# Issuing every engine's instructions in source order in a decode-attention kernel

## The chip, the cores and the metric

The kernel runs on one core of one Trainium2 chip. A core has a matrix engine (TensorE, PE in the profile, with PEld for its weight loads), a vector engine (VectorE, DVE), an activation engine (ScalarE, ACT), GpSimd (POOL) and a sync engine (SyncE, SP) that here issues the loads. Every engine works through one list of its own instructions, and waits at each for the semaphores that the instruction names. The metric is the device time of one execution in microseconds (us); three executions of the kernel before took 269.32 to 269.83 us, with a median of 269.36 us.

## The reference: what is computed

One token of each of two sequences (B = 2, model width D = 448) goes through a layer with two parallel branches, both fed by the normalised input:

```
xn  = layernorm(x)
q   = xn @ wq                                   # 16 query heads of 256
A   = softmax(q . k^T / 16) . v, then @ wo      # last 4096 cached positions, 8 KV heads
h   = xn @ w1 + b1
B   = (h * tanh(softplus(h))) @ w2              # hidden width 1792
out = x + A + B
```

Two query heads share one KV head. K and V are cut to the last 4096 of 32768 positions, which is 4096 x 256 bf16 numbers for each of 8 KV heads, 2 sequences, K and V: 67.1 MB. With the weights 77.67 MB are read. The output is 2 x 448 numbers.

## The kernel before, in words

**Steps.** There are 16 (KV head, sequence) pairs, and each is cut into two halves of 2048 positions: 32 steps. In the source one pass of the loop at L427 does the following for step `s`: it asks for a later K and V (`load_k(s + 3)`, `load_v(s + 1)`), turns the next step's K (`turn(s + 1)`), makes this step's scores (`scores(s)`) and then works on the values of the step before (`values(s - 1)`). At the 4th pass the dense weights are asked for, at the 10th and 12th the dense branch is computed.

**One step's chain of data.** `load_k` (L303) brings 1 MB of K. `turn` (L330) is a DVE transpose of it in 32x32 blocks (`kt<-k`). `scores` (L339) is eight PE matmuls of 128x512 with the spread-out query `qdiag` as weights (`sc<-kt,qdiag`); ACT then takes the exponential and its row sums (L349, `p<-sc`). `values` transposes the probabilities on DVE (L362, `pT<-p`) and multiplies them with V, which serves as weights, in 32 small PE matmuls (L384, `o<-pT,v`). After a pair's second half two matmuls sum the denominators (L371, `den`), DVE takes the reciprocal (L379) and scales the result (L397, `oT`); after both sequences of a KV head four matmuls add it, through `wo`, to the output sum `psA` (L408). The dense branch is L246 to L278, and its second matmul, into the same `psA`, L283.

**Buffers.** K and V have six tiles each, the turned K three, the probabilities, their transposes, the scores and the attention sums two each. A load into a tile waits until its last reader is through: K's last reader is the `turn` on DVE six steps earlier, V's the value matmuls on PE six steps earlier.

**What sets the order.** The program is written with the Tile framework. It notes which instruction reads and writes what; at the end a scheduler takes the instructions out of a heap by priority and decides for each engine in which order they stand, within these dependencies; semaphores are put in after that. So an engine's list needs not follow the source. SP's list before has the same order as the source: K three steps ahead, V one step ahead. Each load also waits for the load eight places before it in the list of loads, so at most eight are under way.

Of the kernel before, what the change touches and what calls it, by code (L numbers as in the profile page):

```python
# [11 lines left out]
BF16 = mybir.dt.bfloat16  # L12
FP32 = mybir.dt.float32
PSUM = bass.MemoryType.PSUM


@with_exitstack
def kernel(
# [49 lines left out]
    small = ctx.enter_context(tc.tile_pool(name="small", bufs=3))  # L68
    ps_sc = ctx.enter_context(tc.tile_pool(name="ps_sc", bufs=2, space=PSUM))
    ps_o = ctx.enter_context(tc.tile_pool(name="ps_o", bufs=2, space=PSUM))  # L70
    ps_den = ctx.enter_context(tc.tile_pool(name="ps_den", bufs=1, space=PSUM))
    ps_a = ctx.enter_context(tc.tile_pool(name="ps_a", bufs=1, space=PSUM))
    ps_m = ctx.enter_context(tc.tile_pool(name="ps_m", bufs=2, space=PSUM))

# [375 lines left out]
    nc.vector.tensor_copy(out=res[:, 0 : D // 2], in_=psA[:, 0 : D // 2])  # L450
    nc.scalar.copy(out=res[:, D // 2 : D], in_=psA[:, D // 2 : D])
    nc.sync.dma_start(out=out.flatten_outer_dims(), in_=res[:])


# [28 lines left out]
```

## Time and profile before

| | before |
|---|---|
| median of 3 runs | 269.36 us (269.32 to 269.83) |
| profiled execution, its own time | 269.08 us |
| span of that execution (first to last instruction) | 267.3 us |
| mean granted TensorE clock | 0.66 |
| PE busy | 167.8 us, 63% of the span |
| DVE busy | 103.8 us, 39% |
| ACT, POOL busy | 25.4 us, 26.8 us |
| read from memory | 77.67 MB, 291 GB/s over the span |

The profiled execution lies 0.28 us under the median, and 1.78 us of its time lie outside the span. Busy time is a sum over stages; how long an engine sat idle, and on whom, is in the views of waits and of groups of instructions. A profile names an instruction by its source line; lines of the changed kernel are 17 higher, since a function of 17 lines stands ahead of them.

### The profile page before, as it was taken

What the parts mean: (1) busy time and instruction counts of PE and PEld (TensorE: products, weight loads), DVE (VectorE), ACT (ScalarE), POOL (GpSimd) and SP (SyncE); (2) the same over time, 40 slices, a digit from 0 to 9 for tenths busy, and PEclk for the clock granted to TensorE, in tenths of its full rate; (3) what the DMA queues carried; (4) which work ended last, traced back from release to release, by engine and by line L of the source; (5) the groups of instructions that cost most, each with busy time, mean ns of one, the idle gap of its engine ahead of it and who ended that gap; (6) DMA issues with size and microseconds to landing.
All of it is one profiled execution on the core that took longest, in us unless ns stands there. A gap on an engine that the chain in (4) does not pass through costs nothing.

```text
span 267.3 us, 3777 instructions
## 1 busy us (share of the span) xinstructions
PE 167.8 (63%) x1577; PEld 80.4 (30%) x1577; DVE 103.8 (39%) x137; ACT 25.4 (10%) x69; POOL 26.8 (10%) x138
## 2 busy tenths in 40 slices
PE   1259557758447895584557865584576955575765
PEld 0233313326213342242123332241232321232323
DVE  5166442241542244634435044634325144444221
ACT  4002111011011011111111101111110011111100
POOL 5043020020020020202020100202020020000000
PEclk9999855557575586579575557568565557559556
DMA  7999999999999999699887966699886914400000
GB/s 278 417 420 418 417 418 427 415 412 421 423 412 422 418 400 343 264 337 362 312 316 265 363 215 223 264 348 350 310 283 237 362 67 157 157 2 0 0 2 0
DMA packets 12554, 77.90 MB, mean 291 GB/s; under 512 B 1269, under 2 KB 3321, under 8 KB 4090
## 3 DMA queue, kind: packets, MB, share of 16 engines
q1 hardware_dynamic: 12532, 77.67, 75.4%
q8 instruction: 12, 0.20, 0.3%
q14 instruction: 4, 0.03, 0.0%
q10 hardware_dynamic: 6, 0.01, 0.0%
HBM read 77.67 MB, written 0.00 MB: 291 GB/s over the span
## 4 chain that ended last, share of the span: by engine, by line
PE 58%; DVE 25%; issue 8%; DMA 4%; ACT 3%; SPq 0%; ACTq 0%; DVEq 0%
PE sc L339 39%; DVE kt L330 20%; PE o L384 10%; DMA wq_sb<-in_A_wq_dram 4%; PE psA L408 4%; DVE pT L362 4%; ACT p L349 3%; PE den L371 1%; PE psA L283 1%; PE hT_ps L246 1%; PE qT_ps L192 1%; PE hT_ps L255 1%; DVE rec L379 0%; DVE qrep L207 0%; SPq L86 0%
## 5 line engine op out<-in xcount | busy, mean ns | idle before, releaser
L339 PE MATMUL sc<-kt,qdiag 128*128 128x512 bf16 x256 | 109.1, 569 | 62.5 <-DVE kt L330 47.3
L330 DVE STREAM_TRANSPOSE kt<-k 128x2048 f32<-128x2048 f32 x32 | 72.3, 2275 | 0.0
L362 DVE STREAM_TRANSPOSE pT<-p 128x512 bf16<-128x512 bf16 x32 | 22.7, 711 | 107.0 <-ACT p L349 104.8
L339 PEld LDWEIGHTS <-qdiag 128*128 128x128 bf16 x256 | 26.2, 122 | 100.2 <-issue 68.2
L221 POOL COPY qdiag<-qrep 32x8 bf16<-32x8 bf16 x128 | 23.0, 185 | 188.3 <-PE sc L339 170.5
L349 ACT ACTIVATE p<-sc 128x512 bf16<-128x512 f32 x32 | 19.1, 597 | 228.0 <-PE sc L339 228.0
L384 PEld LDWEIGHTS <-v 128*128 128x128 bf16 x1024 | 33.6, 104 | 15.0 <-issue 13.2
L384 PE MATMUL o<-pT,v 128*128 128x2 bf16 x1024 | 32.2, 165 | 0.0
L371 PE MATMUL den<-hsel,rs 128*128 128x2 f32 x64 | 15.1, 305 | 22.6 <-ACT p L349 22.6
L371 PEld LDWEIGHTS den<-hsel,rs 128*128 128x128 f32 x64 | 12.5, 242 | 45.8 <-ACT p L349 45.6
L397 DVE TENSOR_TENSOR oT<-o,rec 128x4 bf16<-128x4 f32 x16 | 2.6, 165 | 36.9 <-PE o L384 36.9
L408 PE MATMUL psA<-wo,oT 128*2 128x448 bf16 x32 | 10.8, 478 | 0.3 <-DVE oT L397 0.3
L192 PE MATMUL qT_ps<-xs,wq_sb 128*128 128x4 bf16 x112 | 3.3, 166 | 5.8 <-DMA wq_sb<-in_A_wq_dram 5.8
L349 ACT ACTIVATION_READ_ACCUMULATOR p<-sc 128x1 f32 x32 | 6.2, 194 | 0.0
L192 PEld LDWEIGHTS <-wq_sb 128*128 128x128 bf16 x112 | 3.1, 104 | 6.4 <-DMA wq_sb<-in_A_wq_dram 6.4
L408 PEld LDWEIGHTS <-oT 128*2 128x2 bf16 x32 | 2.4, 94 | 7.9 <-DVE oT L397 5.0
L283 PE MATMUL psA<-w_sb,act_bf 128*2 128x448 bf16 x14 | 3.7, 413 | 0.0
L246 PE MATMUL hT_ps<-xs,w_sb 128*128 128x4 bf16 x49 | 3.7, 195 | 0.0
L146 PE MATMUL xnT_ps<-ident,xn_bf 2*128 2x2 bf16 x7 | 0.5, 166 | 5.0 <-DVE xn_bf L131 5.0
L246 PEld LDWEIGHTS <-w_sb 128*128 128x128 bf16 x49 | 3.2, 151 | 0.1
L201 DVE CAST qT<-qT_ps 128x64 bf16<-128x64 f32 x1 | 0.2, 225 | 7.2 <-PE qT_ps L192 7.2
L110 POOL MEMSET qdiag<- 128x1024 bf16 x3 | 2.7, 951 | 0.0
(40 smaller groups left out, 20.3 us busy)
## 6 DMA issues: line engine op xcount, KB each, us to landing
k<-in_A_k_cache_dram SPq DMA_DIRECT2D x32, 1024.0 KB, 9.8
v<-in_A_v_cache_dram SPq DMA_DIRECT2D x31, 1024.0 KB, 7.4
wo<-in_A_wo_dram SPq DMA_DIRECT2D x8, 448.0 KB, 18.1
w_sb<-in_B_w_dram SPq DMA_DIRECT2D x2, 1568.0 KB, 22.8
wq_sb<-in_A_wq_dram SPq DMA_DIRECT2D x1, 2048.0 KB
wq_sb<-in_A_wq_dram SPq DMA_DIRECT2D x1, 1536.0 KB, 10.9
v<-in_A_v_cache_dram SPq DMA_DIRECT2D x4, 256.0 KB, 3.4
x_bf<-in_A_x_dram ACTq DMA_DIRECT2D x1, 1.8 KB
```

What stands on the lines that cost most here:

```text
L110: nc.gpsimd.memset(t[:], 0.0)
L192: nc.tensor.matmul(qT_ps[:, hh, e, :], lhsT=wq_v[:, s, hh, e, :], rhs=xs[:, s, :, :].rearrange("p x b -> p (x b)"), start=(s == 0), stop=( ...
L221: nc.gpsimd.tensor_copy(out=tv[rows, :, e, j * Q : j * Q + rep], in_=qrep[rows, :, h0 : h0 + rep, e, x, b],)
L246: nc.tensor.matmul(hT_ps[:, c, :, :].rearrange("p x b -> p (x b)"), lhsT=w1_v[:, s, c, :], rhs=xs[:, s, :, :].rearrange("p x b -> p (x b)" ...
L283: nc.tensor.matmul(psA[:, :], lhsT=act_bf[:, c, x, :], rhs=w2_sb[:, x, c, :], start=False, stop=False, skip_group_check=True,)
L330: nc.vector.transpose(out=kt[:].bitcast(FP32), in_=k_t.pop(s)[:].bitcast(FP32))
L339: nc.tensor.matmul(psc[:], lhsT=qdiag[i % NW][:, n * NE + e, :], rhs=ktv[:, n, e, :, :], start=(n == 0 and e == 0), stop=(n == NB - 1 and ...
L349: nc.scalar.activation(out=p_sb[:], in_=psc[:].rearrange("p t c -> p (t c)"), func=ACT.Exp, scale=scale, accum_out=state["rs", i][:, s % N ...
L362: nc.vector.transpose(out=pT[:], in_=p_t.pop(s)[:])
L371: nc.tensor.matmul(den[:], lhsT=rs[:, n : n + 1].to_broadcast([P, P]), rhs=hsel[:], start=(n == 0), stop=(n == NH - 1),)
L384: nc.tensor.matmul(po[:, c, :], lhsT=vv[:, t, c, :], rhs=pTv[:, t, 0:rep], start=(half == 0 and t == 0 and c == 0), stop=(half == NH - 1 a ...
L408: nc.tensor.matmul(psA[:, :], lhsT=oT[:, c, h, :], rhs=w[:, h, c * D : (c + 1) * D], start=False, stop=(kvh == Hkv - 1 and h == rep - 1 an ...
```

## The change

A new function walks over all recorded instructions in the order in which the source made them. To each it adds a dependency on the instruction before it on the same engine, of the kind that needs no semaphore. The scheduler then has no choice left: each engine's list is the source order. The function is called once, as the last statement of the kernel. No instruction is added to the program or taken out of it, no buffer, wait count or size is edited.

```diff
+def issue_in_order(tc):
+
+    last = {}
+    for ins in tc.nc.cur_bb.bb.instructions:
+        before = last.get(ins.engine)
+        if before is not None:
+            tc.add_manual_dep(
+                ins,
+                before.name,
+                mybir.DependencyInfo(
+                    mybir.DependencyClass.NoSync, mybir.DependencyReason.DATA
+                ),
+                reason="issue_in_order",
+            )
+        last[ins.engine] = ins
...
     nc.sync.dma_start(out=out.flatten_outer_dims(), in_=res[:])
+    issue_in_order(tc)
```

**DVE in the loop.** This is DVE's list in the middle of the loop, before. Numbers behind names tell the tiles of different steps apart; `p_1174` are the probabilities of the scores made from `kt_1101`, `p_1234` those from `kt_1163`, `p_1293` those from `kt_1223`.

```order
L330 STREAM_TRANSPOSE kt_1101<-k_954 128x2048
L362 STREAM_TRANSPOSE pT_1176<-p_1112 128x512
L397 TENSOR_TENSOR oT_1019<-o_1040,rec_1120 128x4
L362 STREAM_TRANSPOSE pT_1237<-p_1174 128x512
L330 STREAM_TRANSPOSE kt_1163<-k_1021 128x2048
L379 RECIPROCAL rec_1242<-den_1239 128x2
L362 STREAM_TRANSPOSE pT_1295<-p_1234 128x512
L330 STREAM_TRANSPOSE kt_1223<-k_1087 128x2048
```

And this is the same place in the changed kernel.

```order
L347 STREAM_TRANSPOSE kt_1163<-k_1021 128x2048
L379 STREAM_TRANSPOSE pT_1176<-p_1112 128x512
L347 STREAM_TRANSPOSE kt_1223<-k_1087 128x2048
L379 STREAM_TRANSPOSE pT_1237<-p_1174 128x512
L396 RECIPROCAL rec_1242<-den_1239 128x2
L414 TENSOR_TENSOR oT_1276<-o_1178,rec_1242 128x4
L347 STREAM_TRANSPOSE kt_1282<-k_1159 128x2048
L379 STREAM_TRANSPOSE pT_1295<-p_1234 128x512
```

Before, the K of the next scores (`kt_1163`) is turned behind the transpose of the probabilities of the scores before them (`p_1174`). Now that same K stands two transposes of probabilities earlier, ahead of `pT_1176`, and `oT` follows its reciprocal directly and stands ahead of the next `turn`.

**PE in the loop.** This is PE's list before; of a run of like rows the first or last is shown, and "..." stands for the others. `sc_1225` and `sc_1284` are the scores of two successive steps, and `pT_1237` are the probabilities of the step before `sc_1225`.

```order
L339 MATMUL sc_1225<-kt_1163,qdiag1_131 128x512
L371 MATMUL den_1360<-hsel_124,rs_1235 128x2
L339 MATMUL sc_1284<-kt_1223,qdiag1_131 128x512
...
L384 MATMUL o_1178<-pT_1237,v_1089 128x2
L339 LDWEIGHTS qdiag1_131
L339 MATMUL sc_1284<-kt_1223,qdiag1_131 128x512
```

The changed kernel, one step later in the program:

```order
L356 MATMUL sc_1346<-kt_1282,qdiag2_133 128x512
L388 MATMUL den_1360<-hsel_124,rs_1235 128x2 x2
L401 LDWEIGHTS v_1213
L401 MATMUL o_1297<-pT_1358,v_1213 128x2
...
L425 MATMUL psA_164<-wo_759,oT_1276 2x448
L356 LDWEIGHTS qdiag2_133
L356 MATMUL sc_1408<-kt_1344,qdiag2_133 128x512
```

Before, the values lie in the middle of a later step's eight score matmuls, and a denominator matmul, which needs the row sums of the scores just made, stands between two steps' scores. Now the eight scores stand together, both denominator matmuls follow the scores of the next step, and `psA` follows the values directly.

**DVE at the start.** Before:

```order
L118 BN_STATS stats<-x_bf 2x6
L120 BN_AGGR mv<-stats 2x2
L125 RECIPROCAL rstd<-rstd 2x1
L131 TENSOR_SCALAR xn_bf<-x_bf,mv,rstd 2x4x128
L131 TENSOR_SCALAR xn_bf<-x_bf,mv,rstd 2x3x128
L97 COPY spread<-ident 32x32 x16
```

The changed kernel:

```order
L114 COPY spread<-ident 32x32 x16
L118 CAST hsel<-ident 128x2
L120 TENSOR_TENSOR hsel<-hsel,ident 128x2 x3
L131 MEMSET eps_t 2x1
L135 BN_STATS stats<-x_bf 2x6
L137 BN_AGGR mv<-stats 2x2
```

The constants `spread` and `hsel` now stand ahead of the layer norm. SP's list, and so the order of all loads, is the same in both kernels. On ACT the dense branch's exponential moves from behind the 7th to behind the 10th exponential of scores.

## The prediction

> **What bounds the kernel now.** First the page's slices of the span, for a first picture: who is busy when.
>
> ```profile
> span 267.3 us, 3777 instructions
> PE   1259557758447895584557865584576955575765
> PEclk9999855557575586579575557568565557559556
> DMA  7999999999999999699887966699886914400000
> ```
>
> PE is half busy all along, at a clock that is mostly at half. The DMA engines are full for some 100 us, then not. The loads are thus not what sets the end. The stretches say it in numbers (columns: length, busy time and count of PE, PEld, DVE, ACT, POOL, clock, DMA share, GB/s).
>
> ```profile
> 0.00:7.00 7.00, 0.95 (x8) 0.41 (x8) 3.87 (x25) 2.86 (x3) 3.84 (x10) 1.00 0.77 284
> 7.00:100.00 93.00, 60.54 (x594) 31.12 (x595) 35.01 (x46) 7.10 (x21) 11.18 (x64) 0.69 1.01 417
> 100.00:210.00 110.00, 70.22 (x621) 32.27 (x620) 45.26 (x44) 10.31 (x30) 10.35 (x56) 0.64 0.84 303
> ```
>
> From 7 to 100 us loads run at 417 GB/s; then at 303. The waits of SP's queue (total us, times, longest) say why they fall.
>
> ```profile
> SPq L314 <- PE o L384: 66.2, 22, 9.1
> SPq L303 <- DVE kt L330: 53.4, 11, 5.4
> ```
>
> Loads wait for tiles: V for the value matmuls, K for the turn. Compute is the slow side, and the chain of waits shows how one step goes.
>
> ```profile
> 129.92 0.04 DVE pT L362
> 129.96 0.60 issue
> 130.56 2.28 DVE kt L330
> 132.88 1.89 PE sc L339 x4
> 134.77 0.83 PE o L384 x32
> 135.60 1.57 PE sc L339 x4
> 137.22 0.47 issue
> 137.69 0.20 ACT p L349
> 137.91 0.71 DVE pT L362
> ```
>
> One step takes 137.91 - 129.92 = 7.99 us, and everything in it is in series: transpose of probabilities, turn of the next K, scores, exponential, transpose. The groups (busy, mean ns of one, idle before and its releaser) confirm it.
>
> ```profile
> L339 PE MATMUL sc<-kt,qdiag 128*128 128x512 bf16 x256 | 109.1, 569 | 62.5 <-DVE kt L330 47.3
> L330 DVE STREAM_TRANSPOSE kt<-k 128x2048 f32<-128x2048 f32 x32 | 72.3, 2275 | 0.0
> L362 DVE STREAM_TRANSPOSE pT<-p 128x512 bf16<-128x512 bf16 x32 | 22.7, 711 | 107.0 <-ACT p L349 104.8
> ```
>
> The turn never waits (0.0 idle before it): its K landed long ago, and it starts when the transpose of probabilities ahead of it in DVE's list is done. DVE sits 107.0 us at that transpose, waiting for ACT, with a turn behind it that could run. Then PE waits for the turn. The order of DVE's list, not data, closes the ring.
>
> **The change part by part.**
>
> *The turn moves ahead (DVE), the values behind whole scores (PE).* In the new order the turn for step s+1 stands in front of the transpose for step s-1, and PE does scores(s), then values(s-1). While PE makes scores(s), DVE turns and transposes; nothing of one step's series of 7.99 us remains in series except as fill. What a step costs now is the largest of three rates, per KV head (four steps). For PE I need the durations at both clocks.
>
> ```profile
> 236.27 2.60 PE sc L339 x6
> 240.01 0.89 PE sc L339 x4
> 150.25 1.58 PE psA L408 x4
> 153.58 0.59 PE L371 MATMUL den<-hsel,rs 128*128 128x2 f32 x2 [0.78 <-ACT p L349]
> 242.07 0.46 PEld L408 LDWEIGHTS <-oT 128*2 128x2 bf16 x4 [0.42 <-DVE oT L397]
> ```
>
> At half clock a score matmul is 2.60/6 = 0.433 us, at full clock 0.89/4 = 0.22. PE at half: 32 scores 13.9, four values at 0.83 = 3.3, two pairs of den 1.2, psA 1.58 and the wait for oT in front of it, now uncovered, 0.42: 20.4 us per head. DVE: four turns 9.1, four transposes 2.8, and under 0.7 for rec and oT: 12.6 us. Its new head-of-line wait, oT for the values on PE, holds the next turn back, but that turn is needed only a step later: after oT come 2.28 + 0.71 = 3.0 us to the next values, under 8 x 0.433 = 3.5 us of scores at half clock (at full clock PE would wait about a microsecond; it then has time). Loads: eight of 1.0486 MB and one wo of 0.459 MB, 8.85 MB at 417 GB/s = 21.2 us per head. So the loads become the bound, by 0.8 us over PE at half clock.
>
> The clock: in the chain above PE's longest wait in the step is the turn's, 132.88 - 130.56 = 2.3 us, and in the slices the clock still sits at half for most of the span. I do not count on the full clock. [...]
>
> *What the loads then take.* 284 GB/s x 7 us = 1.99 MB in the first 7 us; the other 75.68 MB at 417 GB/s take 181.5 us: to 188.5 us. A load lands a little after its bytes' turn:
>
> ```profile
> 1.20 10.86 DMA wq_sb<-in_A_wq_dram
> 12.11 3.05 PE qT_ps L192 x108
> 18.57 1.44 PE sc L339 x3
> ```
>
> wq (3.67 MB) had landed at 12.06, when 1.99 + 2.11 = 4.10 MB had moved: 0.43 MB or 1.0 us of lag. The last V lands at T = 189.5 us. Could the loads still be held? K is asked for three steps ahead into six tiles, so load_k(s+3) waits for turn(s-3), and for the load eight places before it, about K(s-1); while the turns follow the landings within two steps, 10.6 us, no load waits for a tile. The dense branch is such a delay:
>
> ```profile
> 63.27 0.49 PE L246 MATMUL hT_ps<-xs,w_sb 128*128 128x4 bf16 x7
> 67.66 0.26 PE L255 MATMUL hT_ps<-ones,b_sb 1*128 1x2 bf16 x2
> L283 PE MATMUL psA<-w_sb,act_bf 128*2 128x448 bf16 x14 | 3.7, 413 | 0.0
> ```
>
> It takes 4.65 us and, at half clock with psA's 1.58/4 a matmul, 14 x 0.395 = 5.5 us, but its weights also gave PE 3.21 MB = 7.7 us in which no K came. It fits.
>
> *The end.* Behind K(31) in the list are three V loads, 3.15 MB = 7.5 us. So K(31) lands at T - 7.5, is turned by T - 5.2, pT(29) ends at T - 4.5, values(29) at T - 3.7, scores(31) at half clock at T - 0.2, exponential (0.7) and pT(31) (0.71) at T + 1.2, values(31) at T + 2.0. From there it is the old end:
>
> ```profile
> 262.69 0.18 DVE oT L397
> 262.91 1.48 PE psA L408 x4
> 265.18 0.33 SPq L452 DMA_DIRECT2D out_dram<-res  x1
> ```
>
> 267.3 - 262.7 = 4.6 us. Span: 189.5 + 2.0 + 4.6 = 196.1 us; with scores at full clock 1.89 instead of 3.46, 194.5.
>
> *The start.* spread and hsel (DVE) move ahead of the layer norm.
>
> ```profile
> 5.09 1.62 DVE L97 COPY spread<-ident 32x32 bf16<-32x32 bf16 x16
> 7.60 0.34 DVE L162 TENSOR_SCALAR xs<-xnT_ps,odd 128x6 bf16<-128x6 bf16 x2
> ```
>
> That is 1.62 + 0.17 + 0.45 = 2.2 us ahead of xs, which is ready at 7.94 and needed, with wq, at 12.06: 4.1 us of cover. Zero. Without cover it would be 2.2 us on PE's start, still under the loads. PE's first scores stay at 18.57. ACT's and POOL's lists have 0.8 and under 1 us per step: zero.
>
> *Sum.* The profiled execution has 269.08 - 267.3 = 1.78 us outside the span: 196.1 + 1.8 = 197.9. The median lay 0.28 above the profiled execution; **I predict 198 us**, 26% less.
>
> **The rivals.**
>
> *PE's ring decides (A).* PE stays at half clock and each hand-over costs more than in my sum. PE's sum without loads: 18.6 + 8 x 20.4 + 4.65 + 5.5 + 4.6 = 197, already level with the loads; 0.1 to 0.3 us per step for hand-overs and 2 to 4 us of DVE standing at the dense branch give 201 to 210 us, say 205 with the outside. For: the chain's "issue" pieces of 0.47 us. Against: where PE had no pause it was granted nearly the full clock (0.91):
>
> ```profile
> 95.00:100.00 5.00, 5.00 (x52) 2.41 (x50) 2.95 (x3) 0.00 (x0) 0.65 (x4) 0.91 0.99 388
> ```
>
> *The loads are slower than 417 (B).* After 100 us the DMA engines were 84% busy for 303 GB/s, 303/0.84 = 361 GB/s of busy time, where the early stretch gives 417/1.01 = 413. If that is the rate of transfers beside dense compute, and not an artefact of few loads under way, then 75.68 MB / 361 = 210 us, T = 217.7, time 226. Against: in the early stretch PE was as busy (60.54 of 93 us against 70.22 of 110) and the rate held. [...]
>
> *Slower than before (C).* DVE's list now has a turn, which needs a K from memory, ahead of the transpose of probabilities that are ready. If K is late, values wait, V tiles stay taken, and SP, stuck at the V load, does not ask for the next K. Such a ring would pay a whole K load per step:
>
> ```profile
> k<-in_A_k_cache_dram SPq DMA_DIRECT2D x32, 1024.0 KB, 9.8
> ```
>
> 18.6 + 32 x 9.8 + 4.6 + 1.8 = 339 us. It beats 269 from (267.3 - 18.6 - 4.6)/32 = 7.6 us per step on, that is, if a K is asked for less than 9.8/7.6 = 1.3 steps before its turn. Against: it is asked for three steps ahead, and six tiles allow it.
>
> *The order was not what held it (D).* 269 us, if the turn needs something that comes late anyway. The 0.0 idle ahead of the turn and the DVE rows speak against it.
>
> **How the numbers follow.** Forecast (loads bound, 195 to 201): 0.70. A (201 to 210): 0.17. B (210 to 230): 0.07. C: 0.03. D: 0.03. The range from 194.5 to 208 takes in the forecast, both clocks, a load rate from 425 to 400 GB/s (-3 to +8 us) and most of A. A measurement of this kernel tells 0.2% from no change. Faster: 0.70 + 0.17 + 0.07 = 0.94; with D split into 0.02 same and a sliver either way, faster 0.95, same 0.02, slower 0.03.
>
> **What would show it.** Right: the DMA slices at 9 up to about 188 us with about 417 GB/s; SP's waits are for other loads, those for PE o and DVE kt nearly gone; turns now sit idle waiting for DMA k; PE's idle time ahead of scores no longer goes to DVE kt behind pT; the last V lands some 6 us before the span's end. A shows as PE near 9 in every slice, SP again waiting for PE o, and a clock at 0.5. B shows as a DMA share of 1.0 at about 360 GB/s. C shows as K loads issued one at a time. I am wrong about the step if PE and DVE still alternate while loads wait.

## The result, and the profile after

The changed kernel takes 199.02 us in the median of four executions (197.60 to 199.63), the kernel before beside it 269.36; the ratio is 0.738 with a 95% interval of 0.733 to 0.743. Medians here and below leave out executions more than 1.5% above the fastest of their kernel, here one of four of the kernel before (273.73 us). The forecast was 198 us. The profiled execution, the fastest of the four, took 197.60 us with a span of 195.8.

First the slices of the page of the changed kernel, and its stretches (columns as in the prediction).

```profile
span 195.8 us, 3758 instructions
PE   0253955699108789999997597489962976597983
PEclk9999999658855756657999969955885698769696
DMA  6999999999999999999999999999999999999950
```

```profile
7.00:100.00 93.00, 67.26 (x733) 38.53 (x734) 47.35 (x60) 10.75 (x29) 11.73 (x73) 0.78 1.01 418
100.00:180.00 80.00, 59.96 (x688) 33.98 (x687) 46.88 (x48) 11.01 (x32) 9.18 (x56) 0.81 1.02 419
180.00:196.00 16.00, 10.90 (x158) 6.76 (x156) 6.58 (x11) 2.40 (x7) 0.00 (x0) 0.79 0.55 221
```

The DMA engines are full to about 188 us, at 418 and 419 GB/s, where they fell to 303 before. SP's waits and the groups show the reversal.

```profile
SPq L320 <- DMA v<-in_A_v_cache_dram: 50.1, 24, 2.2
SPq L331 <- DMA k<-in_A_k_cache_dram: 46.4, 22, 2.3
SPq L331 <- PE o L401: 1.1, 4, 0.3
```

```profile
L347 DVE STREAM_TRANSPOSE kt<-k 128x2048 f32<-128x2048 f32 x32 | 73.7, 2306 | 50.6 <-DMA k<-in_A_k_cache_dram 50.5
L356 PE MATMUL sc<-kt,qdiag 128*128 128x512 bf16 x256 | 83.9, 485 | 2.7 <-DVE kt L347 2.7
L379 DVE STREAM_TRANSPOSE pT<-p 128x512 bf16<-128x512 bf16 x32 | 21.5, 672 | 1.7 <-ACT p L366 1.7
```

Loads now wait for earlier loads; the wait for value matmuls fell from 66.2 to 1.1 us. The turn, which never waited, now waits 50.5 us for K to land. PE's wait for turns fell from 47.3 to 2.7 us, DVE's wait for exponentials from 104.8 to 1.7. The end of the chain of waits:

```profile
164.91 18.67 DMA k<-in_A_k_cache_dram
...
183.61 2.31 DVE kt L347
185.92 0.59 DVE pT L379
...
186.58 0.93 PE o L401 x32
187.50 1.77 PE sc L356 x8
...
189.30 0.70 ACT p L366 x2
...
190.02 0.71 DVE pT L379
...
190.79 0.94 PE o L401 x32
...
191.76 0.18 DVE oT L414
```

The last K lands at 183.6, and from there a chain of single steps leads to the end.

### The profile page after: what moved, and what is told of

The parts are those of the page before. It is cut to its first block, busy times and chain, and to the rows that moved or that the text cites. A ratio compares the mean times of both kernels' runs of the same rounds, so it can differ in the third digit from the quotient of the medians.

```text
span 195.8 us, 3758 instructions
## 1 busy us (share of the span) xinstructions
PE 138.1 (71%) x1577; PEld 79.3 (40%) x1577; DVE 105.9 (54%) x137; ACT 25.4 (13%) x69; POOL 24.7 (13%) x138
## 4 chain that ended last, share of the span: by engine, by line
DMA 89%; DVE 5%; PE 3%; SPq 1%; ACT 1%; issue 0%
DMA k<-in_A_k_cache_dram 40%; DMA v<-in_A_v_cache_dram 30%; DMA wo<-in_A_wo_dram 19%; DVE kt L347 4%; PE o L401 1%; DVE pT L379 1%; PE sc L356 1%; SPq L320 1%; PE psA L425 0%; ACT p L366 0%; SPq L104 0%; SPq L103 0%; DVE res L467 0%; ACT res L468 0%; DVE rec L396 0%
## 5 line engine op out<-in xcount | busy, mean ns | idle before, releaser
L347 DVE STREAM_TRANSPOSE kt<-k 128x2048 f32<-128x2048 f32 x32 | 73.7, 2306 | 50.6 <-DMA k<-in_A_k_cache_dram 50.5
L356 PE MATMUL sc<-kt,qdiag 128*128 128x512 bf16 x256 | 83.9, 485 | 2.7 <-DVE kt L347 2.7
L401 PE MATMUL o<-pT,v 128*128 128x2 bf16 x1024 | 30.7, 164 | 39.0 <-DVE rec L396 20.0
L401 PEld LDWEIGHTS <-v 128*128 128x128 bf16 x1024 | 31.7, 100 | 46.6 <-DMA v<-in_A_v_cache_dram 36.7
L238 POOL COPY qdiag<-qrep 32x8 bf16<-32x8 bf16 x128 | 20.9, 185 | 135.4 <-PE sc L356 120.3
L379 DVE STREAM_TRANSPOSE pT<-p 128x512 bf16<-128x512 bf16 x32 | 21.5, 672 | 1.7 <-ACT p L366 1.7
L425 PE MATMUL psA<-wo,oT 128*2 128x448 bf16 x32 | 9.6, 433 | 2.1 <-DVE oT L414 2.1
L388 PE MATMUL den<-hsel,rs 128*128 128x2 f32 x64 | 9.9, 259 | 0.0
L114 DVE COPY spread<-ident 32x32 bf16<-32x32 bf16 x16 | 3.9, 762 | 1.8 <-POOL spread L110 1.8
L396 DVE RECIPROCAL rec<-den 128x2 f32<-128x2 f32 x16 | 2.3, 143 | 4.2 <-PE den L388 4.1
## 6 DMA issues: line engine op xcount, KB each, us to landing
k<-in_A_k_cache_dram SPq DMA_DIRECT2D x32, 1024.0 KB, 18.5
v<-in_A_v_cache_dram SPq DMA_DIRECT2D x31, 1024.0 KB, 18.5
wo<-in_A_wo_dram SPq DMA_DIRECT2D x8, 448.0 KB, 18.5
```

The costliest lines, as they stand in the source:

```text
L114: nc.vector.tensor_copy(out=spread[rows, b4, j * Q : (j + 1) * Q], in_=ident[rows, rows])
L238: nc.gpsimd.tensor_copy(out=tv[rows, :, e, j * Q : j * Q + rep], in_=qrep[rows, :, h0 : h0 + rep, e, x, b],)
L347: nc.vector.transpose(out=kt[:].bitcast(FP32), in_=k_t.pop(s)[:].bitcast(FP32))
L356: nc.tensor.matmul(psc[:], lhsT=qdiag[i % NW][:, n * NE + e, :], rhs=ktv[:, n, e, :, :], start=(n == 0 and e == 0), stop=(n == NB - 1 and ...
L379: nc.vector.transpose(out=pT[:], in_=p_t.pop(s)[:])
L388: nc.tensor.matmul(den[:], lhsT=rs[:, n : n + 1].to_broadcast([P, P]), rhs=hsel[:], start=(n == 0), stop=(n == NH - 1),)
```

## Experiments

In what follows a turn is called late if, in DVE's list, it stands behind the transpose of the probabilities of the scores right before its own. Counted in the lists, 24 of 32 turns are late in the kernel before, none in the changed one. The ring is the chain that a late turn closes: scores, exponential, transpose, turn, and only then the next scores. Times are medians; the ratio is to the kernel before in the same comparison.

### Which engine's list does it?

Two kernels hold one engine alone to source order; the scheduler picks the others' lists.

```diff
+PINNED = (mybir.EngineType.DVE,)      # the other kernel: mybir.EngineType.PE
...
     for ins in tc.nc.cur_bb.bb.instructions:
+        if ins.engine not in PINNED:
+            continue
```

DVE alone:

> Only DVE's list is held to source order; PE's list is picked by the scheduler and keeps the values in the middle of a later step's scores, as before. Theory (the turn's place in DVE's list made the ring): with the turn ahead of the transposes the ring is open, the loads bound, about 199 us (197 to 203). Rival (PE's order made it: the denominator matmul between two steps' scores and the split scores): most of the 269 stays, 240 or more.

198.15 us, ratio 0.736 (0.729 to 0.743): all of the gain, with none of the turns late, while PE's list still has the values in the middle of scores. PE's order is not what gained.

PE alone:

> Only PE's list is held to source order; in DVE's list, as the scheduler then makes it, about two turns in four still stand behind the transpose of the scores just made. Theory (DVE's order): a step with such a turn costs 3.5 scores + 0.7 exponential + 0.7 transpose + 2.3 turn = 7.3 us, the others 5.1, on average 6.2: 18.6 + 32 x 6.2 + 10 dense + 5 end + 1.8 = 234 us (220 to 250). Rival (PE's order): about 199.

206.70 us, ratio 0.764 (0.754 to 0.773): outside the theory's 220 to 250, and not the rival's 199 either. With PE pinned the scheduler also makes another list for DVE: 13 turns are late instead of 24. The expectation assumed 16 late steps, priced the steps between at 5.1 us, as if at half clock, and added 10 us for the dense branch. From the starts of the 32 exponentials, the 13 late steps took 7.7 us in the mean, as priced, but the 18 others 4.3, with the dense branch in them. In the trace (timeline) two such steps' scores start 3.1 us apart; their eight matmuls take 2.46 and 1.89 us, as against 3.57 in a later step, and the slices of the page have the clock at 0.8 there:

```profile
118.69 2.46 PE L361 MATMUL sc<-kt,qdiag 128*128 128x512 bf16 x8
121.79 1.89 PE L361 MATMUL sc<-kt,qdiag 128*128 128x512 bf16 x8
127.40 3.21 PE L361 MATMUL sc<-kt,qdiag 128*128 128x512 bf16 x8 [2.58 <-DVE oT L419]
134.42 3.57 PE L361 MATMUL sc<-kt,qdiag 128*128 128x512 bf16 x8 [3.03 <-DVE kt L352]
141.33 3.08 PE L361 MATMUL sc<-kt,qdiag 128*128 128x512 bf16 x8
```

Four steps take 141.33 - 118.69 = 22.6 us, 1.4 above the loads' 21.2: about 11 us over eight heads, near the 8 us by which it trails the changed kernel. The run tells that the lists hang together in the scheduler, so pinning PE alone does not isolate PE's part. For that DVE's list has to be set by hand.

### Setting the number of late turns by hand

All engines stay in source order and PE's list stays scores first, values of the step before behind; only the place of the turn in the source changes. In the first kernel every turn is late.

```diff
+        nc.vector.transpose(out=pT[:], in_=p_sb[:])    # at the end of scores(s)
...
-        if s + 1 < NSTEP:
-            turn(s + 1)
         if s < NSTEP:
             scores(s)
+        if s + 1 < NSTEP:
+            turn(s + 1)
```

> All engines in source order, but the source is changed so that the transpose of the probabilities of scores(s) stands ahead of turn(s + 1) on DVE; PE's list keeps its order (scores whole, values of the step before behind them). Theory: the ring is closed again, 7.3 us a step: 18.6 + 32 x 7.3 + 10 + 5 + 1.8 = 269 us (245 to 275; lower where PE's clock is full). Rival (source order as such, or PE's order, is what gains): about 199.

267.26 us, ratio 0.991 (0.986 to 0.996), within the expectation's range. With source order on every engine nearly all of the time is back. Its chain shows the ring, whole, in 138.77 - 131.46 = 7.31 us:

```profile
131.46 0.71 DVE pT L374
132.17 2.19 DVE kt L347
134.37 0.07 DVE rec L397
134.43 3.60 PE sc L356 x8
...
138.08 0.47 issue
138.55 0.20 ACT p L366
...
138.77 0.71 DVE pT L374
```

Two more make three turns in four and one in four late, each behind both transposes that are then ready, as the scheduler had it.

```diff
+        late = s % 4 in (0, 1, 2) and s + 1 < NSTEP     # the other kernel: (1,)
-        if s + 1 < NSTEP:
+        if s + 1 < NSTEP and not late:
             turn(s + 1)
         if s < NSTEP:
             scores(s)
+        if late:
+            if s >= 1:
+                prob_t(s - 1)                           # transpose, once
+            prob_t(s)
+            turn(s + 1)
```

> All engines in source order, PE's list as in the changed kernel; in three steps of four the turn stands behind the transpose of the scores just made, as in the scheduler's DVE list before. Theory (DVE's order makes the ring, PE's order adds to it): three steps at 7.3 us and one at 4.5 are 26.4 us per KV head, over the loads' 21.2: 18.6 + 8 x 26.4 + 10 + 5 + 1.8 = 246 us (238 to 255); the other 23 us of the kernel before then belong to PE's list. Rival (DVE's order alone makes all of it): 265 to 272.

238.77 us, ratio 0.883 (0.878 to 0.888): within the theory's range, at its lower end.

> As the run with three steps of four, but with one late turn in four. Theory (the larger of two rates counts, not their sum): 7.3 + 3 x 4.2 = 19.9 us per KV head, under the loads' 21.2, so the late turn is hidden: 199 us (197 to 204). Rival (each late turn costs its own wait of about 3 us): 199 + 8 x 3 = 223.

200.34 us, ratio 0.741 (0.738 to 0.744): the late turns are hidden.

| kernel | late turns | PE's list | time, us |
|---|---|---|---|
| changed | 0 | source | 199.02 |
| DVE alone pinned | 0 | scheduler | 198.15 |
| one in four | 8 | source | 200.34 |
| PE alone pinned | 13 | source | 206.70 |
| three in four | 24 | source | 238.77 |
| before | 24 | scheduler | 269.36 |
| every turn | 31 | source | 267.26 |

Up to 8 late turns the loads cover them; from 13 on compute is the slower of the two. PE's list costs nothing with no late turn (198.15 against 199.02), but 31 us with 24 (269.36 against 238.77). The 24 late steps are not the same ones in these two kernels, and `rec` and `oT` stand elsewhere in DVE's list, so the 31 us belong to PE's list in the main, not proven to the last.

Where they arise is seen from step to step. From the starts of the exponentials, the 24 late steps took 203.3 us in all in the kernel before and 183.3 with three turns in four late: 20 us. The chain of before, quoted in the prediction, has 0.83 us of values between two halves of the scores, inside the ring, and 24 x 0.83 is 20 us. The 7 other steps took 34.4 against 23.9 us: 10.6 us. There the `den` matmul between two steps' scores counts, since it waits for ACT's row sums. The chain of before shows it:

```profile
145.47 0.02 issue
...
145.99 0.20 ACT p L349
...
146.23 0.59 PE den L371 x2
146.82 1.73 PE sc L339 x4
```

From the end of one step's scores at 145.47 to the next at 146.82 pass 1.35 us; 7 x 1.35 is 9.5 us. In the late step that the prediction quotes `den` costs nothing: the pair, at 129.94 (0.59 us), ran beside DVE's transpose at 129.92 and its turn. These two sums are an account, not runs of their own.

### Are the loads the bound now?

The changed kernel with half of the V loads left out: the second half of each pair uses the first half's V.

```diff
+        if half == 1:
+            v_t[s] = v_t[s - 1]
+            return
...
-        v = v_t.pop(s)
+        v = v_t[s]
```

> The changed kernel, but the second half of each pair uses the V of the first half, so 16 V loads (16.8 MB) are left out and the output is not the reference's. Everything else is done as before. Theory (the loads bound it): the loads end near 7 + 58.9 MB / 0.417 = 148 us, and the time falls by more than 20 us, to between that end (155) and PE's own sum at half clock (195); since a PE without waits was granted the full clock, about 170. Rival A (PE's ring at half clock is level with the loads): 195 or more, next to no change.

162.90 us, ratio 0.604 (0.602 to 0.606), 36 us less than the changed kernel with the same work on PE, DVE and ACT. 16.8 MB at 418 GB/s are 40.1 us, so nine tenths of what the loads saved came out at the end. In its chain the last K lands at 148.67 us, 34.9 earlier than in the changed kernel, and the span, 160.8 us, is 35.0 shorter. In its late stretch PE keeps up with loads that still run at 418 GB/s:

```profile
100.00:145.00 45.00, 40.07 (x585) 25.01 (x582) 38.33 (x40) 8.94 (x26) 6.60 (x40) 1.00 1.02 418
```

PE is busy for 40.07 of 45 us at a granted clock of 1.00. (The full clock in the expectation was 0.91 in the 5 us that the prediction shows.) The opposite test leaves out four of eight score matmuls and keeps the loads.

```diff
-            for e in range(NE):
+            for e in range(1):
...
-                    stop=(n == NB - 1 and e == NE - 1),
+                    stop=(n == NB - 1),
```

> The changed kernel with every second score matmul left out (four of eight per step; the output is not the reference's). Theory (the loads bound it, PE does not): PE's 84 us of score matmuls halve, and the time stays within 197 to 200; only the last scores, 0.9 us less at full clock, show. Rival A (PE's ring is level with the loads): 180 or less.

198.08 us, ratio 0.734 (0.731 to 0.737): half of PE's largest group gone, and no change that these runs resolve.

### Does the lead of the loads matter?

Two tiles for K and V instead of six each.

```diff
-    k_pool = ctx.enter_context(tc.tile_pool(name="kk", bufs=6))
-    v_pool = ctx.enter_context(tc.tile_pool(name="vv", bufs=6))
+    k_pool = ctx.enter_context(tc.tile_pool(name="kk", bufs=2))
+    v_pool = ctx.enter_context(tc.tile_pool(name="vv", bufs=2))
```

> The changed kernel with two K tiles and two V tiles instead of six each, so that load_k(s + 3) waits for turn(s + 1) and load_v(s + 1) for values(s - 1). Theory (the source order costs nothing because the loads run far ahead of the turns): with two of each kind under way a load's own 5 us and more come into the ring, the loads fall below 417 GB/s, about 225 us (205 to 260). Rival C as priced, a whole K load of 9.8 us in each step: about 339. Rival (run-ahead does not matter): 199.

208.74 us in one execution, 10 us more than the changed kernel. SP now waits 73.4 us for turns and 39.0 for values, yet the loads still reach 382 GB/s in the early stretch and 416 in the late one. First its waits, then its early and late stretch:

```profile
SPq L320 <- DVE kt L347: 73.4, 30, 8.1
SPq L331 <- PE o L401: 39.0, 30, 2.6
```

```profile
7.00:100.00 93.00, 62.78 (x707) 36.56 (x708) 44.54 (x56) 10.67 (x29) 11.77 (x72) 0.76 0.95 382
100.00:190.00 90.00, 69.39 (x740) 37.20 (x738) 51.44 (x51) 11.40 (x34) 9.28 (x56) 0.73 1.01 416
```

Lead does matter, but the time lies near the lower end of the range of 205 to 260, far under the 225, and nowhere near rival C's 339. The 36 GB/s that the early stretch lacks against 418 are 3.3 MB in 93 us, or 8 of the 10 us. A K load took 8.8 us from issue to landing in the median (18.5 in the changed kernel); at 416 GB/s that is 3.7 MB under way, so by this estimate some three to four loads were under way while the DMA share was 1.01.

### What stands behind the last load

After the last K come 12.2 us. Three kernels ask for K earlier, two of them also turn it a step earlier.

```diff
-    KA, VA = 3, 1
+    KA, VA = 5, 1          # the third kernel: 4, 1
...
-        if s + 1 < NSTEP:
-            turn(s + 1)
+        if s + 2 < NSTEP:       # second and third kernel, with turn(1) ahead of the loop
+            turn(s + 2)
```

> The changed kernel with K asked for five steps ahead instead of three, so that five V loads instead of three stand behind the last K in the list of loads. Theory: the last K lands 5 us earlier, its turn, scores and transposes are done before the last V lands, and behind the last V come only its last eight matmuls, oT, psA and the output: the end comes 2 to 3 us earlier, 196.5 us. Rival (asking for K so early holds the loads, since load_k(s + 5) waits for turn(s - 1)): 200 or more.

200.30 us, ratio 0.741 (0.738 to 0.743): no gain. In its trace the turns of the last two steps stood behind oT, hence the next kernel.

> The run with K five steps ahead gained nothing, and its trace shows why: the last two turns stood in DVE's list behind oT, which waits for values and so for V, though their K had landed. Here K is asked for five steps ahead and turned two steps ahead of its scores instead of one. Theory (the last steps' chain on DVE and PE sets the end, not the last landing): behind the last V are left values(31), oT, psA and the output; 2 to 3 us less than the changed kernel, 196.5 us (195 to 198). Rival (what follows the last load cannot be shortened by order): 199 or more.

200.07 us, ratio 0.740 (0.735 to 0.745): again none.

> As the run before it, with K four steps ahead, so four V loads behind the last K. Theory: K(31) lands 10 us ahead of the last V, time enough to turn it in its step: the same 196.5 us (195 to 198). Rival: 199 or more.

198.49 us, ratio 0.734 (0.731 to 0.738); 198.0 to 198.8 in six executions lie within the changed kernel's own 197.6 to 199.6. So it is not shown to be faster. The chain of the last one shows why the theory of the end falls:

```profile
170.87 2.31 DVE kt L347
173.18 0.61 DVE pT L379
...
173.82 0.99 PE o L401 x32
174.82 3.44 PE sc L356 x8
...
178.90 0.98 PE o L401 x32
...
181.78 2.72 PE sc L356 x8
184.50 0.78 PE o L401 x32
185.27 1.75 PE sc L356 x8
...
187.37 0.80 PE o L401 x32
188.17 1.77 PE sc L356 x8
```

The turn two steps ahead now waits for its K, landed at 170.84, in front of a transpose that the values need. So PE comes to the values ahead of the last four steps' scores at 173.8 us, where the changed kernel came to the same place at 171.46, and is then busy 15.82 of 16.10 us, up to 189.9. What was taken off the last K was put onto PE. Whether a shorter end can be had by other means stays open.

### The start

```diff
-        nc.gpsimd.memset(t[:], 0.0)
+        nc.vector.memset(t[:], 0.0)
```

> The changed kernel with the three memsets of qdiag on DVE, behind the 16 copies into spread, instead of on POOL. In the changed kernel one of these copies took 2662 ns and ended when POOL's memsets did. Theory (the copy was held by POOL's memsets): the 16 copies take 1.6 to 2.2 us instead of 3.95, the longest under 0.3 us; the time stays at 197 to 200, since the start is covered by the loads. Rival (the long copy has another cause, such as the start of the DMAs): one copy of 2 us or more remains.

198.85 us in one execution. The 16 copies took 1.64 us, the longest 171 ns, against 3.95 us and 2662 ns in the changed kernel (last section). The time is as expected, too.

## Why the prediction was right

**What bounded the kernel before.** "The order of DVE's list, not data, closes the ring" is shown: DVE's list alone opens it (198.15), and putting the turn back closes it under source order (267.26). What the prediction did not see is that the ring's cost had two parts. It described PE's move as part of the same step; the runs show that PE's list is worth nothing without late turns and about 31 us with 24 of them.

**The loads' time.** 417 GB/s held: 418 and 419. The 425 at the fast end of the prediction's range no run shows over a long stretch; what was measured there is 417 before and 418 and 419 after. The bytes were through at 180 + 3.54 MB (16 us at 221 GB/s) / 419 = 188.4 us; forecast 188.5.

**PE against the loads.** The sum of 20.4 us per head at half clock against 21.2 for loads was the tight spot. It was too dark, since the clock rose with the change: from 22 us on (the record of the clock begins about there), its mean was 0.78 against 0.63, and as every entry of that record is either 1.00 or 0.50, it was full for more than half of that time in the changed kernel. So rival A was further off than the sum made it. With 16.8 MB less to load the same work takes 162.9 us, where A's sum had 197 us for PE alone. Why the clock rose is not shown; it did so although PE now has longer idle stretches behind the start than before, up to 9.1 us (at 49.6), where before one was 4.0 us and the others at most 2.7.

**The end.** K(31) landed at 183.6 us (forecast T - 7.5 = 182.0), values(31) ended at 191.7 (191.5), from oT to the end 195.8 - 191.8 = 4.0 (4.6). The last K was 1.6 us later, and the last scores ran at full clock, 1.77 us instead of 3.46: two misses of opposite sign. That the span came to 195.8 against a forecast of 196.1 is thus partly luck, and it is the fastest execution's; the others' spans were 196.9 to 197.8.

**The start.** Priced at 2.2 us under 4.1 of cover. xs was ready at 9.82 instead of 7.94 us, 1.9 later, so the sum looks right and is not. The prediction's own rows have the copies ahead of xs before the change too (5.09 against 7.60), so the move alone should have added little. Two other things made the 1.9: the copies took 3.95 instead of 1.62, while the layer norm, which had waited until 2.74 us for x, no longer had to. The cover held; PE's first scores began at 18.46 (18.57 before).

**The rivals.** B fell: no loss of rate beside denser compute (418 and 419 GB/s with PE busy for 67.26 of 93 and 59.96 of 80 us). C's mechanism exists but its price was wrong. A whole K load per step assumed one load under way at a time; even with two tiles some three to four are under way by the estimate above, and the cost is 10 us. D fell with the result.

## What to carry to other kernels

Where an engine idles at an instruction that waits, look at what stands behind it in its list and could run: here a 2.3 us transpose whose input had long landed stood behind one that waited for the step just made, 24 times of 32, and three engines paid for it in series. Pinning order is not the remedy in itself: a list in source order with that transpose in the wrong place was within 1% of the scheduler's time (267.26 us, ratio 0.991). And count the ring's and the loads' time per round, not the waits: here 8 late turns of 32 left the time at 200.34 us against 199.02, where 24 brought it to 238.77.

## What the runs showed of the hardware

**A DVE copy held for the whole of POOL's memsets.** The changed kernel's copies into spread (DVE) began while POOL cleared three qdiag tiles. First the timeline:

```profile
1.71 2.74 POOL L127 MEMSET qdiag<- 128x1024 bf16 x3
1.80 3.95 DVE L114 COPY spread<-ident 32x32 bf16<-32x32 bf16 x16 [1.80 <-POOL spread L110]
```

And the view of the line (shortest, median and longest in ns, then when the first and the last began):

```profile
L114 DVE COPY spread<-ident x16: 156/164/2662, 1.8 to 5.6; 32x32 bf16<-32x32 bf16 x16
```

The line's first copies, begun at 1.80, hold the 2662 ns and come free when POOL's third memset ends, at 4.45; the others took about 164 ns. With the memsets on DVE the longest was 171 (one execution). The hold outlasted not one memset of about 0.9 us but three in a row. How POOL's memsets hold a DVE copy, no run shows. The kernel before shows that not every DVE instruction is held: its batch-norm statistics began at 2.74, beside the same memsets, and took 0.62 us, as against 0.61 in the changed kernel at 6.45, with the memsets done.

**The granted clock did not follow busy time.** In the changed kernel three stretches in a row have PE busy throughout by the records, at three different mean clocks:

```profile
74.40:77.80 3.40, 3.40 (x51) 2.25 (x50) 0.32 (x1) 0.69 (x2) 1.32 (x8) 0.66 0.99 401
77.90:81.30 3.40, 3.40 (x49) 3.25 (x47) 0.00 (x0) 0.00 (x0) 0.00 (x0) 0.82 1.04 422
81.30:84.70 3.40, 3.40 (x12) 1.41 (x11) 2.66 (x7) 0.23 (x1) 0.00 (x0) 0.50 1.02 424
```

Most of the middle stretch is the dense branch's matmuls of 4 columns and fewer; scores of 512 columns stand before and behind it. By the microsecond the clock was 0.50 from 67 to 76 us, 1.00 from 77 to 80, and 0.50 again from 81 to 90: it rose behind scores (0.65 in the microsecond from 76) and fell while only narrow matmuls ran (0.55 in that from 80). What sets the clock in such a mix is not shown.
